# Clearing the convolution's input tile with GpSimd, and loading x for it in four transfers

## The chip, the cores and the metric

The kernel runs on one core of one Trainium2 chip. The metric is device microseconds of one execution, the median of several runs; lower is better.

## The reference

Two branches share the work, and a gate mixes them. `x` has 2048 rows of 448 channels, in bfloat16, and is the input of both; all weights are bfloat16.

```python
g = sigmoid((x * gate_w).sum(-1, keepdims=True))
# A: attention with 16 heads of 28, one key head and one value head for all
q = (x @ wq) -> 16 heads;  k = x @ wk;  v = x @ wv
p = softmax(q k^T * 28 ** -0.5);  a = (p v) @ wo
# B: a state-space convolution along the rows; 256 complex states for each channel
K[d, l] = Re(sum_n C[d, n] * exp(dt[d] * A[d, n] * l) * dt[d] * B[d, n])
y = causal convolution of x and K along l, by channel (the reference uses FFTs);  b = y + x * Dskip
out = g * a + (1 - g) * b
```

## The kernel before, in words

The attention runs as 1024 score tiles: 16 groups of 64 (a group is a block of 512 queries and 4 heads). For each tile TensorE makes 128 keys by 512 queries in PSUM (L1373 from four row strips, `qT`, or L1396 from the zero-padded copy `qM`). ScalarE takes the exponential of two or three tiles at once into the ring `expT` (L1428, 410 of them). TensorE then multiplies by the values into the bank `psB` (L1449, four tiles at a time). At a group's end VectorE copies `psB` to `acc` (L1173), and only then may the next group's first L1449 write the bank. TensorE also multiplies by zeros where it would be idle (L1349, L1355, L731).

The queries of each group are projected by TensorE (L893, L902) and moved out by VectorE (L899, L905); GpSimd issues four transfers that spread them from `qT` to `qM`.

The convolution runs beside this. VectorE squares complex numbers (the masters, L934 to L954) and builds tables of powers (L974 to L1024) in 14 chunks of 32 channels. TensorE makes the convolution's kernel from them (L1047), VectorE copies it to `kstg` (L1059), GpSimd stores it to DRAM (`KP`), and SyncE loads it back as shifted rows: the T loads, mostly into `T`. TensorE multiplies them with `U` (L1114); L1124, L1135 and L1144 turn the result, scale it and add it to `O`.

`U` holds the convolution's input for half of the channels at a time. Each pair of channels has 64 words of four bytes in each partition: the first 16 are rows of x (`in_A_x_dram` in the profile), the other 48 are the same rows moved by 32, 64 and 96 places, with zeros where nothing is moved in. So `U` is first cleared, then the input is loaded to the staging tile `O`, then VectorE copies it into `U` (and the second half of the channels into `T`) at L627, and then transfers from `U` to `U` (`ushift`, 24 issues) make the moved copies. After that a transfer clears `O`, which is used as the output's accumulator from then on.

All instructions are put into order by a planner in the kernel (`Prog.schedule`). Each step is an `op` (or a `dma`) with an engine, an assumed duration, the keys that it reads and writes, and a priority `pr`, lower first. The planner works through time and takes, over all engines, the step that can start first. So an edit in one step moves others on every engine. Waits come from the keys: the last writer of a key that is read, the readers of a key that is written. A `dma` waits for the one before it in the same slot. Steps in `late` may start only after the last store of the transposed x (`XS_scratch`). On GpSimd each computing step waits for the one before it. In the kernel before, `U`'s zero-fill has the key `Uz`, the two groups of eight loads have `("ust", 0)` and `("ust", 1)`, and the moved copies have `("Uc", c)` for a chunk c. All DMA issues have line 164 in the profile, where the helper `dma` records them.

Of the kernel before, what the change touches and what calls it, by code (L numbers as in the profile page):

```python
# [12 lines left out]
P = 128  # L13

S = 2048
D = 448
# [20 lines left out]
UA = D // 2  # L37
# [47 lines left out]
def dram(t, off, dims):  # L85
    return bass.AP(tensor=t.tensor, offset=t.offset + off, ap=[list(d) for d in dims])
# [342 lines left out]
class Kernel:  # L429
# [117 lines left out]
    def loads(self):  # L547
        pg, ins = self.pg, self.ins
        self.xst = self.tab
        x = ins["A_x"]  # L550

        def lx(q):
            pg.dma([(self.xst.v(0, P, q * QS, [[1, 4 * D]]), dram(x, q * 4 * P * D, [[4 * D, P], [1, 4 * D]]))],
                   (128, 3584), f"x{q}", wr=[("xst", q)], fac=0.85)
        self.raw = self.T
        self.late = []
        raw = self.raw
        names = ["B_A_im", "B_A_re", "B_B_re", "B_B_im", "B_C_re", "B_C_im"]

        def lraw(k, eng="sp"):  # L560
            pg.dma([(raw.v(0, DT, k * 1024, [[1, 1024]]), dram(ins[names[k]], 0, [[1024, DT], [1, 1024]]))],
                   (112, 2048), f"raw{k}", wr=[("raw", k)], eng=eng, fac=0.8)
        self.dtb = self.cst
        wst = self.mbf
        wks = self.seedw
        lx(0)
        pg.dma([(self.dtb.v(0, 1, 0, [[1, D]]), dram(ins["B_log_dt"], 0, [[D, 1], [1, D]]))], (1, 896), "ldt", wr=["dt"], eng="act", extra=-1500)
        pg.dma([(wks.v(0, DT, 0, [[1, 112]]), dram(ins["A_wk"], 0, [[112, DT], [1, 112]]))], (112, 224), "wk", wr=["wks"], eng="act")
        lx(1)
        lx(2)  # L570
        lraw(0)
        lx(3)
        pg.dma([(wst.v(0, DT, 0, [[1, 4 * D]]), dram(ins["A_wq"], 0, [[4 * D, DT], [1, 4 * D]]))],
               (112, 3584), "wq", wr=["wqs"], fac=0.85)
        pg.dma([(wks.v(0, DT, 112, [[1, 112]]), dram(ins["A_wv"], 0, [[112, DT], [1, 112]])),
                (wks.v(0, DT, 224, [[1, 4]]), dram(ins["gate_w"], 0, [[4, DT], [1, 4]]))],
               (224, 200), "wv", wr=["wvs"], extra=1500)
        lraw(1)
        pg.op("dve", lambda e: e.tensor_copy(self.Wk.v(0, DT, 0, [[32, 16], [1, DH]]),
                                             wks.v(0, DT, 0, [[DH, 4], [0, 4], [1, DH]])), 300, rd=["wks"], wr=["Wk"])  # L580
        pg.op("dve", lambda e: e.tensor_copy(self.Wq.v(0, DT, 0, [[32, 64], [1, DH]]),
                                             wst.v(0, DT, 0, [[DH, 64], [1, DH]])), 620, rd=["wqs"], wr=["Wq"])
        pg.op("dve", lambda e: e.tensor_copy(self.Wv.v(0, DT, 0, [[32, 4], [1, DH]]), wks.v(0, DT, 112, [[DH, 4], [1, DH]])),
              180, rd=["wvs"], wr=["Wv"], pr=0.3)
        pg.op("dve", lambda e: e.tensor_copy(self.Wv.v(0, DT, 28, [[32, 4]]), wks.v(0, DT, 224, [[1, 4]])),
              100, rd=["wvs"], wr=["Wvg"], pr=0.3)
        V0 = lambda b, off, n, r: b.v(0, P, off, [[n // r, r], [1, n // r]])
        Z = lambda n, r: self.cst.v(0, P, 512, [[0, r], [1, n // r]])
        uc = [("Uc", c) for c in range(14)]
        self.late.append(pg.dma([(V0(self.U, 0, 64 * UA, 64), Z(64 * UA, 64))], (8192, 448), "zU", rd=[("cst", 1)],  # L590
                                wr=["Uz"], pr=0.25).i)
        for k in range(2):
            lst = [(self.O.v(0, P, (8 * k + j) * D, [[1, D]]),
                    dram(x, 32 * (15 - 8 * k - j) * D, [[D, 32], [512 * D, 4], [1, D]])) for j in range(8)]
            self.late.append(pg.dma(lst, (1024, 896), f"u{k}", wr=[("ust", k)], pr=0.3).i)
        for k in range(2, 6):
            lraw(k)
        pg.dma([(V0(self.Wo, 0, NT * D, 8), Z(NT * D, 8))], (1024, 448), "zW", rd=[("cst", 1)], wr=["Wo"], pr=1)
        pg.dma([(self.k0.v(0, 1, 0, [[1, D]]), dram(ins["B_Dskip"], 0, [[D, 1], [1, D]]))], (1, 896), "sk", wr=[("kst", 1)], pr=1)
        w = ins["A_wo"]  # L600
        pg.dma([(self.Wo.v(32 * r, DH, 0, [[D, 4], [1, D]]), dram(w, DH * r * D, [[D, DH], [4 * DH * D, 4], [1, D]]))
                for r in range(4)], (448, 896), "wo", rd=["Wo"], wr=["Wo"], pr=2)
        pg.dma([(dram(self.KP, 2049, [[4 * KW, 112], [KW, 4], [1, 63]]), self.cst.v(0, 112, 512, [[64, 4], [1, 63]]))],
               (448, 126), "pad", rd=[("cst", 1)], wr=["pad"], pr=3)
# [10 lines left out]
    def prep_u(self):  # L615
        pg = self.pg
        done = []
        U4, T4, O4 = (b.cast(mybir.dt.int32) for b in (self.U, self.T, self.O))
        for half in range(2):
            for k in range(2):  # L620
                if half == 0:
                    dst, w = U4.v(0, P, 8 * k, [[64, UA // 2], [1, 8]]), ["Uz", ("Ub", k)]
                else:
                    dst, w = T4.v(0, P, UB // 2 + 8 * k, [[16, UA // 2], [1, 8]]), ["rawdone", ("UB", k)]
                key = ("ustd", half, k)
                done.append(key)
                pg.op("dve", lambda e, dst=dst, k=k, half=half: e.tensor_copy(  # L627
                    dst, O4.v(0, P, (8 * k * D + half * UA) // 2, [[1, UA // 2], [D // 2, 8]])), 1000,
                    rd=[("ust", k)] + ([] if half else []), wr=w + [key], pr=1 + half)
        for k, (c0, c1) in enumerate(((0, 2), (2, 5), (5, 9), (9, 14))):  # L630
            n = 16 * (c1 - c0)
            pg.dma(self.ushift(self.U, 1024 * c0, self.U, 1024 * c0, 128, n, 1), (6 * 16 * n, 64), f"du{k}", rd=[("Ub", 0), ("Ub", 1)],
                   wr=[("Uc", c) for c in range(c0, c1)], pr=0.35 if k < 2 else 0.9 + 0.1 * k, slow=True, iss=700.0)
        V0 = lambda b, off, n, r: b.v(0, P, off, [[n // r, r], [1, n // r]])
        Z = lambda n, r: self.cst.v(0, P, 512, [[0, r], [1, n // r]])
        pg.dma([(V0(self.O, 0, 16 * D, 32), Z(16 * D, 32))], (4096, 448), "zO", rd=[("cst", 1)] + done,
               wr=[(x, q) for q in range(16) for x in ("O", "Oz")], pr=1)
# [911 lines left out]
```

## Time and profile before

| what | value |
|---|---|
| median of 3 runs | 497.94 us (497.27 to 498.53) |
| profiled execution, span from the first to the last instruction | 498.77 us (the page rounds it to 498.8) |
| TensorE busy | 462.3 us (93%) |
| VectorE busy | 458.6 us (92%) |
| ScalarE busy | 484.0 us (97%) |
| GpSimd busy | 183.8 us (37%), nearly all of it issuing DMAs |
| granted TensorE clock, mean | 0.997 |

The profile is one execution; its own time is the span of its instructions, 0.83 us above the median of the runs, which were taken without a profile. A group's row in the page's part 5 gives busy time, mean duration of one in ns and, behind the second bar, the engine's idle time just before those instructions with the engine that ended most of it. A row of a timeline has the start, the busy time, the engine, the line, the operation and the tiles; equal instructions that follow each other are one row with a count, and brackets at the end give the idle time ahead of the row and what ended it. A row on "SPq" is SyncE's queue issuing, and its time is that of the issue alone.

### The profile page before, as it was taken

The numbers are of one execution on the slowest core, as the hardware profiler recorded it, in microseconds if no ns is written. First come the engines' busy times: TensorE is split into PE (matmuls) and PEld (weight loads), VectorE is DVE, ScalarE is ACT, GpSimd is POOL, SyncE is SP. The second block draws the span as 40 slices with busy tenths as digits, with TensorE's granted clock in tenths as the row PEclk, the third lists the DMA queues.
The fourth block names the chain that finished last, engine by engine and source line by source line (L and its number), as shares of the span: only waits on it lengthen the run. The fifth ranks groups of instructions, "written<-read, shape, count | busy, mean of one in ns | idle before, by whom it ended". The sixth has DMA issues, their size and how long they took to land.

```text
span 498.8 us, 17277 instructions
## 1 busy us (share of the span) xinstructions
PE 462.3 (93%) x7559; PEld 207.8 (42%) x7645; DVE 458.6 (92%) x872; ACT 484.0 (97%) x436; POOL 183.8 (37%) x331
## 2 busy tenths in 40 slices
PE   8899899999999999999999999999999999999997
PEld 5432233343443444444334344444534344444444
DVE  6998999999999999999999999999999999995224
ACT  6999899999999999999999999999999999999995
POOL 2102034225232527428616552643743525142110
PEclk9999899999999999999999999999999999999999
DMA  8996686935809555776942963798595695877752
GB/s 242 319 187 159 96 174 103 282 119 160 246 12 283 132 184 141 217 205 155 291 124 50 272 171 85 204 234 207 137 279 141 171 285 131 268 207 230 215 175 71
DMA packets 117479, 91.86 MB, mean 184 GB/s; under 512 B 48698, under 2 KB 112492, under 8 KB 117404
## 3 DMA queue, kind: packets, MB, share of 16 engines
q1 hardware_dynamic: 106746, 78.91, 57.7%
q0 software_dynamic: 10384, 11.70, 9.9%
q8 instruction: 60, 0.98, 0.9%
q10 hardware_dynamic: 274, 0.14, 0.1%
q14 instruction: 15, 0.12, 0.1%
HBM read 73.61 MB, written 5.23 MB: 158 GB/s over the span
## 4 chain that ended last, share of the span: by engine, by line
ACT 85%; SPq 6%; PE 4%; DVE 4%; DMA 1%; issue 0%
ACT expT L1428 84%; SPq L164 6%; DVE tab L988 1%; PE psS L658 1%; DMA O<-in_A_x_dram 1%; DVE tab L1003 0%; PE psS L1373 0%; PE psS L1396 0%; PE psS L1286 0%; PE psB L1349 0%; PE psB L1449 0%; ACT L805 0%; PE psS L1047 0%; DVE expT L680 0%; PE psX L1047 0%
## 5 line engine op out<-in xcount | busy, mean ns | idle before, releaser
L1428 ACT ACTIVATE expT<-psS 128x1536 bf16<-128x1536 f32 (+1 forms) x410 | 464.4, 1409 | 3.8 <-PE psS L1373 2.6
L988 DVE TENSOR_TENSOR tab<-tab,mbf 128x512 bf16<-128x512 bf16 (+4 forms) x140 | 139.4, 999 | 0.0
L1373 PE MATMUL psS<-qT,kT 29*128 29x512 bf16 x684 | 96.1, 386 | 12.0 <-ACT expT L1428 6.9
L1449 PE MATMUL psB<-expT,vaug 128*32 128x512 bf16 x1000 | 100.1, 390 | 2.2 <-DVE acc L1173 1.9
L1396 PE MATMUL psS<-qM,kT 128*128 128x512 bf16 x240 | 78.0, 382 | 13.8 <-issue 7.9
L164 POOL DMA_DIRECT2D KP_scratch<-kstg x104 | 57.1, 556 | 65.1 <-DVE kstg L1059 59.5
L1003 DVE TENSOR_TENSOR tab<-tab 128x256 bf16<-128x256 bf16 (+4 forms) x140 | 77.1, 571 | 0.0
L1449 PEld LDWEIGHTS psB<-expT,vaug 128*32 128x32 bf16 x1000 | 25.7, 93 | 74.9 <-issue 70.7
L164 POOL DMA_DIRECT2D qM<-qT x64 | 32.5, 516 | 59.0 <-DVE qT L905 38.4
L1373 PEld LDWEIGHTS psS<-qT,kT 29*128 29x128 bf16 x684 | 23.7, 91 | 64.3 <-ACT expT L1428 50.9
L164 POOL DMA_DIRECT2D U<-T x49 | 36.6, 750 | 36.2 <-DMA U<-T 14.6
L1355 PE MATMUL psB<-ident,one 128*128 128x512 bf16 x149 | 49.0, 389 | 0.0
L164 POOL DMA_DIRECT2D rdenB<-R_scratch x60 | 31.9, 538 | 34.6 <-DMA R_scratch<-denT 33.8
L1114 PE MATMUL psS<-T,U 128*26 128x128 bf16 (+3 forms) x1856 | 42.8, 221 | 0.5 <-issue 0.3
L1114 PEld LDWEIGHTS psS<-T,U 128*26 128x26 bf16 (+3 forms) x1856 | 32.9, 105 | 16.7 <-issue 11.7
L1017 DVE TENSOR_TENSOR tab<-tab,tmp 128x1984 bf16<-128x1984 bf16 x28 | 32.5, 1185 | 0.1
L1114 PE MATMUL psX<-T,U 128*32 128x128 bf16 (+3 forms) x1408 | 31.6, 221 | 0.0
L1396 PEld LDWEIGHTS psS<-qM,kT 128*128 128x128 bf16 x316 | 19.0, 97 | 30.1 <-ACT expT L1428 20.5
L164 POOL DMA_DIRECT2D denT<-acc x15 | 10.7, 716 | 55.8 <-DVE acc L1173 55.8
L1114 PEld LDWEIGHTS psX<-T,U 128*32 128x32 bf16 (+3 forms) x1408 | 24.3, 105 | 11.0 <-issue 7.4
L1011 DVE TENSOR_TENSOR tmp<-tmp,mq 128x64 bf16<-128x64 bf16 (+4 forms) x70 | 25.2, 360 | 0.0
L934 DVE TENSOR_TENSOR msq<-seedz 128x512 f32<-128x512 f32 (+1 forms) x40 | 24.6, 616 | 0.0
(188 smaller groups left out, 502.9 us busy)
## 6 DMA issues: line engine op xcount, KB each, us to landing
T<-KP_scratch SPq DMA_DIRECT2D x204, 272.0 KB, 4.9
U<-KP_scratch SPq DMA_DIRECT2D x20, 272.0 KB, 6.2
rdenB<-R_scratch POOLq DMA_DIRECT2D x60, 64.0 KB, 3.6
U<-cst SPq DMA_DIRECT2D x1, 3584.0 KB, 25.2
qM<-qT POOLq DMA_DIRECT2D x64, 32.0 KB, 3.7
tab<-in_A_x_dram SPq DMA_DIRECT2D x4, 448.0 KB, 5.3
O<-in_A_x_dram SPq DMA_DIRECT2D x16, 112.0 KB, 3.0
O<-cst SPq DMA_DIRECT2D x1, 1792.0 KB, 9.3
```

The source lines that it names most:

```text
L164: return [e.dma_start(o, i, **kw) for o, i in pairs]
L934: pg.op("dve", lambda e: e.tensor_tensor(m2(msq), z2, z2, ALU.mult), el(2 * n), rd=[kr, ki] + first, wr=["msq"], pr=pr)
L988: mul = lambda e, o, a, b: e.tensor_tensor(o, a, b, ALU.mult)
L1003: vo(lambda e, dv=dv, tv=tv, k=k: e.tensor_tensor(dv, dv, tv, ALU.add if k else ALU.subtract), n, [kt[k], kd[k]], [kd[k]], 1.92 if lv else ...
L1011: vo(lambda e, w=w, lv=lv: e.tensor_tensor(rho.v(0, P, (32 - 2 * w) * 2, [[64, 32], [2, w], [1, 2]]), rho.v(0, P, (32 - w) * 2, [[64, 32], ...
L1017: vo(lambda e, k=k: e.tensor_tensor(tab.v(0, P, FM + k * FP + 2, [[64, 32], [2, 31], [1, 2]]), tab.v(0, P, lm + k * PL + 62, [[64, 32], [- ...
L1114: r = e.matmul(ps.v(32 * j, 32 - m0, 128 * k, [[1, 128]]), self.U.v(0, P, (4 * gi + j) % UA // 2 * 128 + 2 * (2 * m0 + par) + j % 2, [[4, ...
L1355: return e.matmul(t.v(0, P, off, [[1, 512]]), self.one.v(0, P, 2, [[0, P]]), self.ident.v(0, P, 0, [[0, 4], [1, P]]), start=b != 6, stop=b ...
L1373: r = e.matmul(self.psS.v(0, P, 512 * b, [[1, 512]]), kT.v(32 * h, DH + 1, 128 * kt, [[1, 128]]), qT.v(32 * h, DH + 1, 512 * (i % 2), [[1, ...
L1396: return e.matmul(self.psS.v(0, P, 512 * b, [[1, 512]]), kT.v(0, P, 128 * kt, [[1, 128]]), self.qM.v(0, P, (i % 2) * XQ + 512 * h, [[1, 51 ...
L1428: o = pg.op("act", lambda e: e.activation(expT.v(0, P, 512 * es[0], spread(es, n)), self.psS.v(0, P, 512 * bs[0], spread(bs, n)), AF.Exp, ...
L1449: r = e.matmul(self.psB.v(32 * h, 32, 0, [[1, 512]]), vaug.v(0, P, 32 * kt, [[1, 32]]), expT.v(0, P, 512 * ring[t], [[1, 512]]), start=(kt ...
```

## The change

The zero-fill transfer of `U` is taken out. In its place GpSimd clears 14 pieces of `U`, each 8 pairs of channels, and of each pair only the 48 words that VectorE's copy doesn't write. The pieces have the keys `("Uc", c)`, which the moved copies write later. The sixteen transfers of x, one for each column block of `O`, become four, one for each residue of the partition number modulo four: 32 partitions with 16 rows of 448 channels. All four copies at L627 wait for all four transfers. The bytes that are loaded, their place in `O` and the rest of the kernel are the same. Lines behind the edit have numbers higher by one in the changed kernel.

```diff
         V0 = lambda b, off, n, r: b.v(0, P, off, [[n // r, r], [1, n // r]])
         Z = lambda n, r: self.cst.v(0, P, 512, [[0, r], [1, n // r]])
-        uc = [("Uc", c) for c in range(14)]
-        self.late.append(pg.dma([(V0(self.U, 0, 64 * UA, 64), Z(64 * UA, 64))], (8192, 448), "zU", rd=[("cst", 1)],
-                                wr=["Uz"], pr=0.25).i)
-        for k in range(2):
-            lst = [(self.O.v(0, P, (8 * k + j) * D, [[1, D]]),
-                    dram(x, 32 * (15 - 8 * k - j) * D, [[D, 32], [512 * D, 4], [1, D]])) for j in range(8)]
-            self.late.append(pg.dma(lst, (1024, 896), f"u{k}", wr=[("ust", k)], pr=0.3).i)
+        U4 = self.U.cast(mybir.dt.int32)
+        for c in range(14):
+            pg.op("pool", lambda e, c=c: e.memset(U4.v(0, P, 512 * c + 16, [[64, 8], [1, 48]]), 0), 470.0, wr=[("Uc", c)], pr=4)
+        for h in range(4):
+            xs = 4 * self.O.rs
+            pg_pair = (bass.AP(tensor=self.O.h, offset=h * self.O.rs, ap=[[xs, 32], [D, 16], [1, D]]),
+                       dram(x, (512 * h + 32 * 15) * D, [[D, 32], [-32 * D, 16], [1, D]]))
+            self.late.append(pg.dma([pg_pair], (512, 896), f"u{h}", wr=[("ust", h)], pr=0.3).i)
...
                 if half == 0:
-                    dst, w = U4.v(0, P, 8 * k, [[64, UA // 2], [1, 8]]), ["Uz", ("Ub", k)]
+                    dst, w = U4.v(0, P, 8 * k, [[64, UA // 2], [1, 8]]), [("Ub", k)]
...
-                    rd=[("ust", k)] + ([] if half else []), wr=w + [key], pr=1 + half)
+                    rd=[("ust", h) for h in range(4)], wr=w + [key], pr=1 + half)
```

## The prediction

> **What bounds the kernel now.** I read the page's chain of work first, then ScalarE's costliest group in its part 5.
>
> ```profile
> ACT 85%; SPq 6%; PE 4%; DVE 4%; DMA 1%; issue 0%
> L1428 ACT ACTIVATE expT<-psS 128x1536 bf16<-128x1536 f32 (+1 forms) x410 | 464.4, 1409 | 3.8 <-PE psS L1373 2.6
> ```
>
> The 410 exponentials of the attention take 464.4 us on ScalarE, and ScalarE is idle before them for only 3.8 us. So a change can do three things to the time: move the start of this stream, close part of the 3.8 us, or open new gaps. Next, ScalarE's timeline, to see where the 3.8 us lie; the number in brackets is the idle time before the row.
>
> ```profile
> 31.71 2.37 ACT L1428 ACTIVATE expT<-psS 128x1536 bf16<-128x1536 f32 x2 [0.72 <-PE psS L1396]
> 34.23 24.27 ACT L1428 ACTIVATE expT<-psS 128x1536 bf16<-128x1536 f32 x21 [0.16 <-PE psS L1396]
> 59.45 1.02 ACT L1428 ACTIVATE expT<-psS 128x1024 bf16<-128x1024 f32 x1 [0.95 <-PE psS L1373]
> 61.51 2.52 ACT L1428 ACTIVATE expT<-psS 128x1536 bf16<-128x1536 f32 x2 [1.03 <-PE psS L1373]
> 64.39 4.62 ACT L1428 ACTIVATE expT<-psS 128x1536 bf16<-128x1536 f32 x4 [0.36 <-PE psS L1373]
> ```
>
> Two further gaps, 0.23 us at 69.2 and 0.26 us at 80.9, are the last; from 80.9 to 492.0 us nothing starves ScalarE. Everything lost is lost in the first 81 us, where the change lies. Why TensorE was late is in the timelines of SyncE's queue, VectorE and TensorE:
>
> ```profile
> 15.42 1.64 SPq L164 DMA_DIRECT2D U<-cst  x1
> 17.11 31.53 SPq L164 DMA_DIRECT2D O<-in_A_x_dram  x16
> 50.92 0.95 DVE L627 COPY U<-O 128x896 int32<-128x896 int32 x1 [2.99 <-DMA O<-in_A_x_dram]
> 57.93 0.70 DVE L1173 COPY acc<-psB 128x512 f32<-128x512 f32 x1
> 58.69 0.40 PE L1449 MATMUL psB<-expT,vaug 128*32 128x512 bf16 x4 [1.94 <-DVE acc L1173]
> ```
>
> The zero-fill keeps the DMA engines busy, and the first load of x, issued at 17.1, holds the queue 20.7 us. The sixteenth lands at 50.9. VectorE stands 2.99 us for it; all behind it is late, also the copy that frees psB (L1173); TensorE stands 1.94 us for that copy. The windows by five microseconds show what follows (PEclk is third from the end):
>
> ```profile
> 55.00:60.00 5.00, 3.06 (x21) 1.00 (x22) 5.00 (x11) 4.05 (x4) 0.71 (x1) 0.97 0.52 59
> 60.00:65.00 5.00, 4.85 (x26) 1.20 (x26) 5.00 (x7) 3.56 (x4) 0.00 (x0) 0.69 0.95 199
> ```
>
> After its stand TensorE is granted 0.69 of its clock, and that is where the gaps of 1.03 and 0.36 us come from. The gap at 31.7 has another cause. The trace gives its releaser as ScalarE, which had long been done; the answer for tile qM in the window 20.5 to 24 has the real one:
>
> ```profile
> L164 POOL DMA_DIRECT2D qM<-qT x4: 496/496/672, 21.0 to 22.7; - x4
> DMA to landing us min/median/max: 5.7/5.8/8.1
> ```
>
> The last of these four issues, at 22.7, lands 8.1 us later at 30.8, just when TensorE loads its first weights for L1396 (30.83). The next four, at 40.5 us without the zero-fill, land in 2.3 to 2.6 us.
>
> **The change, part by part.** *Removed: the zero-fill.* Its 3584 KB land 25.2 us after issue. Without it the loads of x come right behind the three XS stores (issued last at 14.6, landing after 6.6 to 7.5 us, so at 21.2 to 22.1).
>
> *x in four transfers.* Same 1.84 MB, same 896-byte rows, 4 issues in place of 16; SyncE is through at about 18 us instead of 48. When does the last one land? In the window 40 to 45 us the loads of x moved 223 GB/s at a DMA share of 0.83, so 269 GB/s at a full share: 6.8 us. From 21.4 that is 28.2, and with the 3.0 us from issue to landing of one of these loads as an outer allowance, 31.2. The slow bound is the pace of the sixteen (12 issues in 7.8 us, 177 GB/s): 10.4 us, landing at 34.8. I take 30 to 32.
>
> *VectorE's order.* The listing of the changed program puts the four copies L627 directly behind the second seedw product, which ends at 31.7; in the kernel before they start at 44.9 and 50.9. The first copy now waits for all four transfers. Queued behind it: the reduction L899 for the second q projection, the k0 row (L878) and the whole chain of masters. If x is there at 31.7, the 2.99 us are gone. Up to the copy L1173 the list is otherwise the same plus one small product L1011 (0.13 us apart in the trace): 31.69 + (57.93 - 31.69) - 2.99 + 0.13 = 55.07, done at 55.77. TensorE came to the waiting L1449 at 58.69 - 1.94 = 56.75, now 0.88 us sooner (next item), so at 55.87: no stand, no slow clock. A late x has cover: 1.94 us of standing became a gap of 0.95, so 1.0 us of standing costs nothing directly, and x may land up to about 32.8.
>
> *qM.* The loads of x are out of the DMA engines some 9 us sooner than the zero-fill, so the qM transfers issued at 21.0 to 22.7 should land by 30.3, when TensorE is free (L1349 ends at 30.30): the gaps of 0.72 and 0.16 us close, 0.88. Bounds: 0 if they still take 8.1 us, 0.88 if the 5.8 of their median.
>
> *GpSimd's 14 clears.* Each is 128x384 words of four bytes. Rows of this trace:
>
> ```profile
> 1.34 0.21 POOL L511 MEMSET kstg<- 128x128 f32 x1
> 1.97 0.09 POOL L511 MEMSET expT<- 28x1 bf16 x1
> ```
>
> So 0.12 us for 127 more words, 0.36 for 383 more, 0.45 for one; with 0.07 us between two, 14 take 7.3 us, from 4.5 to 11.8. GpSimd's next work is the qM issue at 21.0, after 16.28 us of idling: that idling hides them; even at twice the length they end at 19. The first shift transfers (U<-U) wait for GpSimd and VectorE, both long done. What they can cost is VectorE's start-up. No row shows GpSimd computing beside a copy between two SBUF tiles on VectorE. Bounds: nothing, or one clear's 0.45 us ahead of each of L579 (5.77), L808 and L831 (11.58). Of the first two's 0.90, TensorE's wait for ScalarE hides 0.49 (VectorE's first xT copy ends at 7.53, L688 starts at 8.06 after ScalarE's at 8.02); the rest, 0.41, passes to kT, L696 and, with L831's 0.45, through L832 to ScalarE's L834, behind which ScalarE is full until the first exponential: 0.86 at most. Nothing here can gain. I take 0.43, the middle.
>
> [...]
>
> *Moved.* The shifts U<-U go from 51.9 to 79 us to about 34 to 53, and the k0 store behind them; the first reader, the convolution's L1114, starts at 96.9, and the first T load at 84.0, so both hide. If the shifts slow the qM transfers at 40.5 to 8 us, their first reader is at 65.0: hidden. Further on the planner has re-ordered all engines (ScalarE's order is the same); I count nothing for that, and keep it as rivals.
>
> **Sum.** Closed: 0.88 + 0.95 + 1.03 + 0.05 (a small one at 63.0) + 0.36 = 3.27 us. Start-up: 0.43 lost. Net 2.84 us. The profiled span of 498.77 becomes 495.93; it lies 0.83 above the median of the runs, 497.94, so the forecast is 495.1 us.
>
> **Rivals.**
> 1. *x still comes late, or one new stand eats the gain* (0.24). At the slow bound, 34.8 us, VectorE stands 3.1 us at 31.7 instead of at 47.9: the gaps at 59 to 64 stay, only qM's 0.88 less 0.43 remains: 497.5. For it: the margin is 1 to 2 us, and a transfer lands with its slowest DMA engine. Against it: the sixteen were paced by issues, at a share under 0.86. A single later stand as long as the present one (2.39 us of gap) also gives 497.5.
> 2. *The new order makes TensorE stand at later changes of the head group* (0.20): slower. Place: the psB copy L1173, which occurs 15 times, each time VectorE's list is a microsecond or two late beside a product of 1.1 to 2.3 us. Price: 2.39 us each by the row at 58.7. From two of them on the gain is gone: 497.94 - 2.84 + 4.78 = 499.9. Against it: in the kernel before, 14 of 15 cost nothing, and all 56 T loads after 80 us landed before use. For it: TensorE's products often end within 0.1 us of the exponential that needs them, so there is little to absorb a bad order.
> 3. *The clears do not run where they seem to.* The listing has all 14 ahead of GpSimd's first DMA; only a clear above 1.1 us would delay qM. I give it no share of its own.
>
> **Chances.** 0.3% (1.5 us) is about what a measurement can tell from no change. Forecast, below 496.4: 0.56, its own range 494.1 (all gaps closed, no start-up cost: 3.8 us off) to 496.4. Within: 0.24. Slower: 0.20. Range for 8 in 10: 494.1 to 499.9, which takes in rival 1 and the near part of rival 2.
>
> **What would show it.** Right: no VectorE idle time before the L627 copies (now at about 32), L1173's copy near 55 and no TensorE stand behind it, PEclk 1.00 from 60 to 65, ScalarE idle before exponentials under 1 us in total, the first exponential at 21.3 to 22.1. Wrong at x: a DMA wait of 2 us or more before L627 at 32. Wrong at start-up: a first exponential after 22.1. Wrong altogether: ScalarE gaps of over 2.8 us in total after 81 us.

## The result, and the profile after

| what | before | changed |
|---|---|---|
| median of 4 runs each, same chip | 497.75 us (497.27 to 498.53) | 504.36 us (501.44 to 506.81) |
| span of the profiled execution | 498.77 us | 504.8 us |
| mean granted TensorE clock of the profiled execution | 0.997 | 0.982 |
| ScalarE idle before the exponentials | 3.8 us | 6.6 us |

The ratio is 1.0128, with a 95% interval of 1.0079 to 1.0176. The forecast was 495.1 us, with 499.9 as its upper end. Medians here and below are over all executions of a kernel; ratios and their intervals leave out executions more than 1.5% above their kernel's fastest.

The first 81 us went as forecast. In VectorE's timeline the copies of x start at 31.70 and the copy that frees psB at 55.02, without a wait for x:

```profile
31.70 1.81 DVE L628 COPY U<-O 128x896 int32<-128x896 int32 x2
...
55.02 0.69 DVE L1174 COPY acc<-psB 128x512 f32<-128x512 f32 x1 [0.22 <-PE psB L1450]
```

In ScalarE's timeline the first exponential starts at 21.26, and up to 68 us only two gaps of over 0.1 us are left:

```profile
21.26 1.44 ACT L1429 ACTIVATE expT<-psS 128x1536 bf16<-128x1536 f32 x1
...
33.52 31.97 ACT L1429 ACTIVATE expT<-psS 128x1536 bf16<-128x1536 f32 x28 [0.16 <-PE psS L1397]
65.72 3.71 ACT L1429 ACTIVATE expT<-psS 128x1536 bf16<-128x1536 f32 x3 [0.23 <-PE psS L1374]
```

The loss is at the other end. The page's clock row falls in the last two slices, and the exponentials' row has more idle time than before, now ended by L1385, a score product of the last head groups:

```profile
PEclk9999999999999999999999999999999999999966
...
L1429 ACT ACTIVATE expT<-psS 128x1536 bf16<-128x1536 f32 (+1 forms) x410 | 465.0, 1393 | 6.6 <-PE psS L1385 5.6
```

ScalarE's timeline from 475 us shows each gap. The last two rows are in the tail, where the results go out.

```profile
475.37 4.80 ACT L1429 ACTIVATE expT<-psS 128x1536 bf16<-128x1536 f32 x4
481.99 2.37 ACT L1429 ACTIVATE expT<-psS 128x1536 bf16<-128x1536 f32 x2 [1.81 <-PE psS L1385]
484.62 2.59 ACT L1429 ACTIVATE expT<-psS 128x1536 bf16<-128x1536 f32 x2 [0.27 <-PE psS L1385]
488.31 1.45 ACT L1429 ACTIVATE expT<-psS 128x1536 bf16<-128x1536 f32 x1 [1.10 <-PE psS L1385]
490.19 1.02 ACT L1429 ACTIVATE expT<-psS 128x1024 bf16<-128x1024 f32 x1 [0.43 <-PE psS L1385]
492.10 1.45 ACT L1429 ACTIVATE expT<-psS 128x1536 bf16<-128x1536 f32 x1 [0.88 <-PE psS L1385]
494.66 0.60 ACT L1429 ACTIVATE expT<-psS 128x512 bf16<-128x512 f32 x1 [1.11 <-PE psS L1385]
499.67 0.38 ACT L1243 ACTIVATE acc<-psB 32x256 f32<-32x256 f32 x1 [4.41 <-PE psB L1444]
502.00 0.54 ACT L1310 ACTIVATE O<-psS 128x448 bf16<-128x448 f32 x1 [1.95 <-PE psS L1287]
```

The six gaps before exponentials add up to 5.60 us. TensorE's timeline shows what came ahead of the first of them: a stand of 1.85 us that no engine and no transfer of the kernel ended ("issue").

```profile
478.99 0.47 PE L1115 MATMUL psX<-T,U 128*32 128x128 bf16 x17
481.31 0.30 PE L1115 MATMUL psX<-T,U 128*28 128x128 bf16 x7 [1.85 <-issue]
```

The windows around it have, behind the length, the busy time of TensorE, of its weight loads, of VectorE, ScalarE and GpSimd, then TensorE's granted clock, the DMA share and GB/s. Over the 3.41 us to 483.49 TensorE is busy for 2.18 us; from then on its clock is half.

```profile
476.66:480.08 3.42, 2.61 (x60) 1.17 (x53) 1.11 (x2) 3.42 (x4) 0.00 (x0) 1.00 0.92 250
480.08:483.49 3.41, 2.18 (x43) 0.96 (x46) 0.00 (x0) 1.60 (x3) 0.00 (x0) 1.00 0.06 18
483.49:486.90 3.41, 3.41 (x52) 1.22 (x56) 1.45 (x3) 3.03 (x3) 0.00 (x0) 0.50 0.00 0
```

The counts tie the stand to the arrival of instructions. The profile's queue "q8 instruction" moves 60 packets with 0.98 MB together, 16 KB each, and TensorE has 15,334 records in the trace: 255.6 for each packet. Numbered by their starts, the only two stands of over 0.5 us ahead of TensorE's products that are put down to "issue" (0.57 us at 177.33, 1.85 us at 481.31) are both at place 193 of 256, 41 times 256 records apart. A block, here, is 256 such records; that one packet brings one block is my reading of these counts. The block before the second one began at 474.29; the next packet of q8 started 4.5 us later, at 478.82, took 1.06 us, and TensorE went on 1.43 us behind its end.

### The profile page after: what moved, and what is told of

Read it like the earlier page. It is cut to its first block, busy times and chain, and to the rows that moved or that the text cites. A ratio compares the mean times of both kernels' runs of the same rounds, so it can differ in the third digit from the quotient of the medians.

```text
span 504.8 us, 17352 instructions
## 1 busy us (share of the span) xinstructions
PE 481.7 (95%) x7637; PEld 210.0 (42%) x7637; DVE 459.1 (91%) x872; ACT 484.6 (96%) x436; POOL 189.6 (38%) x345
## 4 chain that ended last, share of the span: by engine, by line
ACT 86%; PE 8%; issue 1%
ACT expT L1429 86%; PE psX L1115 1%; PE psS L1385 1%; PE psS L1397 1%; PE psS L1374 1%; PE psB L1444 1%; PE psS L1259 1%; PE psB L1350 1%; PE psB L1450 0%; PE psS L1234 0%; PE psS L1219 0%; PE psS L1287 0%; PE psX L1048 0%; PE psS L1048 0%; PE psS L894 0%
## 5 line engine op out<-in xcount | busy, mean ns | idle before, releaser
L1397 PE MATMUL psS<-qM,kT 128*128 128x512 bf16 x316 | 95.2, 384 | 0.8 <-ACT expT L1429 0.3
L1356 PE MATMUL psB<-ident,one 128*128 128x512 bf16 x141 | 46.4, 384 | 0.0
L1115 PE MATMUL psS<-T,U 128*26 128x128 bf16 (+3 forms) x1920 | 42.8, 221 | 0.1
L1115 PEld LDWEIGHTS psS<-T,U 128*26 128x26 bf16 (+3 forms) x1920 | 32.8, 105 | 16.1 <-issue 10.8
L1115 PE MATMUL psX<-T,U 128*32 128x128 bf16 (+3 forms) x1344 | 31.6, 223 | 2.4 <-issue 2.4
L1115 PEld LDWEIGHTS psX<-T,U 128*32 128x32 bf16 (+3 forms) x1344 | 23.6, 106 | 14.2 <-issue 10.0
```

Of the source, the lines that this page charges most:

```text
L1115: r = e.matmul(ps.v(32 * j, 32 - m0, 128 * k, [[1, 128]]), self.U.v(0, P, (4 * gi + j) % UA // 2 * 128 + 2 * (2 * m0 + par) + j % 2, [[4, ...
L1356: return e.matmul(t.v(0, P, off, [[1, 512]]), self.one.v(0, P, 2, [[0, P]]), self.ident.v(0, P, 0, [[0, 4], [1, P]]), start=b != 6, stop=b ...
L1397: return e.matmul(self.psS.v(0, P, 512 * b, [[1, 512]]), kT.v(0, P, 128 * kt, [[1, 128]]), self.qM.v(0, P, (i % 2) * XQ + 512 * h, [[1, 51 ...
```

## The experiments

Theory 1: the new order, which the planner made because of the edit, costs the time, by the late block and the half clock behind it. Theory 2: the edit itself costs it (GpSimd's clears beside VectorE, the four transfers). Theory 3: the half clock at the end comes without the stand, for want of work.

**Another order at the end (a_fetch).** One constant of the planner, the time after which the next block is taken to be there:

```diff
-    else self.FETCH if r < self.QUIET else self.IDLE))
+    else 7400.0 if 468000.0 < r < 474000.0 else self.FETCH if r < self.QUIET else self.IDLE))
```

> The changed kernel with one constant of its planner altered for one place: the block of TensorE instructions that is fetched for 476 us is taken to come 7.4 us after the one before it, where 4.8 us was assumed and the trace of the changed kernel shows 7.02 us (474.29 to 481.31). Only the order at the end of TensorE's list and a few VectorE rows change; GpSimd, SyncE and ScalarE keep theirs. Theory 1 (the loss is TensorE's late instruction block at 479 to 481 us, and the half clock that comes behind it): the 1.85 us stand goes, the half clock of 17.07 us shrinks to the three or four us that the kernel before has, ScalarE's gaps behind 480 us (6.6 us at the exponentials) fall to under 1 us, and the time is 494.5 to 498. Theory 2 (the clears and the x transfers themselves cost it): 501 to 507. Theory 3 (the half clock at the end comes without the stand, for want of work): the stand goes, the half clock stays, 500 to 504.

504.08 us, ratio 1.0103 (1.0057 to 1.0149). The stand at 481 is gone (behind 178 us none that is put down to "issue" is above 0.4), and so is the half clock of 17.07 us. But a half clock of 6.83 us now lies at 375.98, and in the tail ScalarE waits 4.94 us ahead of L1310 in place of 1.95, because the planner moved work there: convolution products (L1115) now run from 494.7 to 496.2 us, behind the last exponential. Theory 1's mechanism held and its time did not: one repair bought other losses. Theory 3's half clock at the end did not stay.

**The same order, blocks shifted (b_shift64, b_shift160).** In the emitting loop, waits that are met long before, 61 in one kernel (limit 64) and 155 in the other (limit 160), each one more instruction:

```diff
+    if e == "pe" and o.end > 100000.0 and extra < 64 and waits and "dve" not in waits:
+        waits = dict(waits, dve=1)
+        extra += 1
```

> The changed kernel in its own order, with 61 waits on VectorE that are long met added to TensorE instructions behind 100 us, each one instruction more, so that TensorE's blocks of 256 instructions end 61 instructions earlier in the work than in the changed kernel. Theory 1: the place where the block ends moves by about a quarter of a block, so the stand of 1.85 us at 481.31 changes in size or is gone, and the time moves with it by 2 us or more, to 495 to 500 if it is gone. Theory 2 and 3: the same 501 to 507 as the changed kernel, since order, clears and transfers are the same.

> As the kernel with 61 added waits, but with 155, so that the blocks of 256 instructions end 155 instructions earlier. Theory 1: the stand at 481.31 is gone or elsewhere, and the time differs from the changed kernel's by 2 us or more, 495 to 500 if no stand falls behind 470 us. Theory 2 and 3: 501 to 507.

500.62 us, ratio 1.0040 (1.0014 to 1.0066), and 500.96 us, ratio 1.0054 (1.0030 to 1.0079). The stand near 480 shrank to 0.57 and 1.06 us, with no half clock behind it in either trace. Order, clears and transfers are those of the changed kernel, so Theory 2 can't explain the 3.4 to 3.7 us that the median fell. What is left lies over other late blocks (0.80 us at 327 in the one, 1.12 us at 451.64 in the other) and half clocks in 10 of the 20 executions.

**Both edits in the old order (c_order).** GpSimd clears, x in four transfers; the planner sees the old costs, and a transfer of 128 bytes to a scratch tensor takes the zero-fill's place in the plan. The first copy also waits for both groups of loads, which the lines shown leave out:

```diff
+    z = pg.dma([(dram(self.ZZ, 0, ...), self.cst.v(0, 1, 512, [[1, 64]]))], (8192, 448), "zU", ..., wr=["Uz"], pr=0.25)
...
+    o = pg.dma(lst, (1024, 896), f"u{k}", wr=[("ust", k)], pr=0.3)
+    o.iss *= 4
```

> The changed kernel's two edits in the order of the kernel before: GpSimd clears U in 14 pieces, the one zero-fill transfer is replaced by one of 128 bytes into a scratch tensor, x comes in four transfers, and the planner is given the old costs, so that TensorE's list is that of the kernel before but for a few filler rows. Theory 1 (the edit itself gains what the prediction summed, and the new order loses it at 481 us): no stand at 480 us, the early gaps of ScalarE closed (3.3 us in the sum), 494 to 496.5 against 497.5 of the kernel before. Theory 2 (the clears and the transfers cost the time): slower than the kernel before, 500 or more. Theory 3: as before or up to 500, with the half clock at the end.

498.07 us, ratio 0.9997 (0.9975 to 1.0020): neither a gain nor a loss, and a mean clock of 0.999 or 1.00 in all ten executions. In its trace ScalarE's early gaps are 0.16, 0.23 and 0.26 us, so x came in time; a block came late there too (1.82 us at 475.46; ScalarE lost 1.60 us by it in this execution, the slowest of the ten), without a half clock. Theory 2 falls, and so does half of Theory 1's expectation: the early gain isn't there.

**The kernel before, once more (before_2).** No edit.

> The kernel before once more, for a second trace. The prediction took the profiled execution (span 498.77 us) as an ordinary one that lies 0.83 us above the median of the times; but the times of the changed kernel lie 1.72 us above their spans, by which the execution with a span of 498.77 would have taken 500.5 us, some 2.8 us above the median of 497.7. Theory A (the profiled execution was an unusual one): in this trace the half clock of 3.41 us at 59.7 us is absent, and ScalarE's gaps of 0.95, 1.03 and 0.36 us at 59 to 64 us add up to under 1 us, with a span of 495.5 to 496.5 us. So 1.5 to 2.3 us of the 2.4 us that the prediction counted as the gain at that place were not there to be gained. Theory B (it was ordinary): the same gaps, 2.3 to 2.5 us in total, whatever the span.

Span 496.6 us, time 498.36 us. Theory A holds, and more so than expected. ScalarE's timeline and VectorE's copies:

```profile
33.52 31.97 ACT L1428 ACTIVATE expT<-psS 128x1536 bf16<-128x1536 f32 x28 [0.16 <-PE psS L1396]
65.72 11.40 ACT L1428 ACTIVATE expT<-psS 128x1536 bf16<-128x1536 f32 x10 [0.23 <-PE psS L1373]
77.39 5.98 ACT L1428 ACTIVATE expT<-psS 128x1536 bf16<-128x1536 f32 x5 [0.27 <-PE psB L1449]
```

```profile
44.67 0.95 DVE L627 COPY U<-O 128x896 int32<-128x896 int32 x1
...
47.65 0.96 DVE L627 COPY U<-O 128x896 int32<-128x896 int32 x1
```

The gaps at 33.52 and 65.72 are those of the changed kernel to the hundredth. Neither copy waits: the loads of x were issued from 15.63 to 44.49 here, from 17.11 to 48.64 in the first profile. The stand of 1.94 us, its half clock and the gaps of 0.95, 1.03 and 0.36 us are in the first profile alone. Over the runs of the kernel before beside these experiments, 81 of 86 executions had a mean clock above 0.998; four had 0.990 to 0.997, a range in which the first profile's 0.997 lies, and one of 660.82 us had 0.559.

The gap of 0.72 us ahead of L1396 is another matter, and the other traces show it. Six traces are of kernels that keep the zero-fill (two of the kernel before, and n_null1, n_null2, g_gaps and d_cross, which are told further down). In three of them the last of the first four qM transfers lands at 30.28 to 30.73 us, and ScalarE has a gap of 0.72, 0.58 (n_null1, with a clock of 1.00) and 0.29 us (d_cross) there; in the other three it lands by 29.95 and there is none. In the eleven traces with GpSimd's clears it lands by 29.88, always without the gap. VectorE's wait for x also comes back, 1.56 us in n_null1, but there no gap of ScalarE follows at 59 to 64 us.

**The changed kernel, once more (after_2).** No edit.

> The changed kernel once more, for a second trace and more times. Theory 1 (late instruction block, then half clock): a stand of TensorE behind no other engine of 1 to 2.5 us at 479 to 482 us in this execution too, 500 to 507 us; executions whose mean clock is 1.00 are at 499 to 501.5, those at 0.98 at 504 or more, so that some 2 us of the loss come from the stand and the order and the rest from the half clock. Theory 2 and 3: the time is spread without a tie to the mean clock, or the stand is absent and the time the same.

504.44 us, ratio 1.0124 (1.0088 to 1.0161). The late block is there again (1.23 us at 483.64), with a half clock of 6.83 us from 484.93; another of 6.83 us starts at 375.70. Over the seven executions of the changed kernel that the ratios use, the times lie along 499.0 us + 423 us x (1 - mean clock), with a correlation of 0.97. Their mean clock is 0.9884: by this fit 4.9 us of the loss go with the half clock. The other 1.5 us, from 497.5 to 499.0, fit the late blocks and the tail; no run here separates these two.

**The new order without the edit's direct part (d_cross).** The changed kernel's plan, with the zero-fill and sixteen loads executed in it; GpSimd's pieces shrink to one element of a small tile.

```diff
-    pg.op("pool", lambda e, c=c: e.memset(U4.v(0, P, 512 * c + 16, [[64, 8], [1, 48]]), 0), 470.0, wr=[("Uc", c)], pr=4)
+    pg.op("pool", lambda e, c=c: e.memset(self.small.v(0, P, 4, [[1, 1]]), 0.0), 470.0, wr=[("Uc", c)], pr=4)
+    z = pg.dma([(V0(self.U, 0, 64 * UA, 64), Z(64 * UA, 64))], (8192, 448), "zU", rd=[("cst", 1)], wr=["Uz"], pr=0.25)
+    z.ns, z.iss = 1.0, 0.0
```

> The other way round from the kernel with the order of the kernel before: the order that the planner made for the changed kernel (TensorE's list differs in 7 rows), but with the direct parts of the kernel before. U is zeroed by the one transfer of 8192 descriptors, the 14 GpSimd pieces shrink to memsets of one element of a small tile, and x comes in sixteen transfers. Theory 1 (the order makes the loss): slow like the changed kernel or slower, 501 to 508, with a late block at 474 to 482 us and the early gaps at 31 us and behind it back. Theory 2 (the clears and the four transfers make it): as the kernel before, 497 to 498.5.

516.56 us, ratio 1.0400 (1.0355 to 1.0444). The late block is there (1.66 us at 501.02, this trace being some 20 us late), so it belongs to the order. The size was missed: VectorE's row shows why.

```profile
49.89 0.93 DVE L633 COPY U<-O 128x896 int32<-128x896 int32 x1 [18.14 <-DMA O<-in_A_x_dram]
```

The new order puts the copies at 31.7 and everything for the second q projection behind them; with x at 49.9, ScalarE stood for 15.10 us. In the changed kernel the last load of x lands at 27.98 us, 21.9 us earlier than here, and the copies start 18.2 us earlier. So the edit does deliver x early. The old order simply did not need it earlier.

**The old order with both edits and shifted blocks (c_shift64).** The 61 waits of b_shift64 in c_order.

> The kernel with both edits in the order of the kernel before, with 61 waits that are long met added on TensorE behind 100 us, so that its blocks of instructions end 61 instructions earlier. In the trace of the kernel without them, a block came 5.42 us late and TensorE stood for 1.82 us at 475.46. Theory 1: the stand there shrinks or moves; if none of over 0.5 us is left behind 400 us, the median falls from 498.07 to 496 to 497, below the kernel before. Against it: the transfers of 466 to 479 us fill the DMA engines, so another block may come as late; then 497.5 to 499. Theory 2: no change from 498.

499.48 us, ratio 1.0052 (1.0032 to 1.0071): a miss for both theories' numbers, and nearest to the sentence against it. The stand at 475 is gone, but a block now comes 1.54 us late at 326.25, and ScalarE loses 1.00 us there. The old order is exposed too. In before_2 its blocks come late by stands of 0.47 us at 326.48, 0.56 at 467.39 and 0.59 at 473.72, for which ScalarE loses 0.17, 0.17 and 0.43 us; it happens to lie well.

**New plans for old work (n_null1, n_null2, m_replan).** Only a figure that the planner assumes is altered: 620 to 720 ns for the copy of Wq in the kernel before and in the changed kernel, 1000 to 900 ns for the copies of x in the kernel before.

```diff
-    wst.v(0, DT, 0, [[DH, 64], [1, DH]])), 620, rd=["wqs"], wr=["Wq"])
+    wst.v(0, DT, 0, [[DH, 64], [1, DH]])), 720, rd=["wqs"], wr=["Wq"])
```

> The kernel before with nothing of its work altered: only the planner is told that one early VectorE copy (the one of Wq, L581) takes 720 ns in place of 620. The instructions are the same, their order is planned anew (1395 lines of TensorE's list differ). Theory 1 (it is the order that came out of the planning that costs the changed kernel its time, so any new planning draws a new order and new late stands): the time moves by more than 0.3%, somewhere between 496 and 504, and the trace shows stands of TensorE of over 0.6 us at other places than the kernel before. Theory 2 (the clears and the transfers cost it): within 0.3% of the kernel before, 496 to 499.

> As the run before it, with another figure altered: the planner is told that the four copies of x (L627) take 900 ns in place of 1000 (the trace shows 945 to 960). Theory 1: a third order with a time of its own between 496 and 504, different from the run before it. Theory 2: 496 to 499.

> The changed kernel with the same false figure for the copy of Wq, so that the same work as in the changed kernel is planned into another order. Theory 1: the time leaves the 504.4 of the changed kernel by 2 us or more, to 496 to 502, and the stand at 479 to 484 us is another or gone. Theory 2: 503 to 505.5 again, since clears and transfers are the same.

n_null1: 499.80 us (497.62 to 503.71), ratio 1.0049 (1.0023 to 1.0075). n_null2: 498.94 us, ratio 1.0037 (1.0013 to 1.0061), with a late block of 1.59 us at 326.87 in its trace. The work is that of the kernel before; only the order differs, and with it the number of dummy products at L1355 (156 in before_2's trace, 157 and 159 in these). Both are slower, by 0.49% and 0.37%, with intervals clear of 1, though n_null2's 498.94 lies in the ranges of both theories. n_null1's trace is of one of its fastest executions (497.85 us) and has neither a late block of over 0.4 us nor a half clock, so what its slower executions lost by isn't shown. m_replan: 503.92 us (499.45 to 508.56), ratio 1.0075 (1.0042 to 1.0109). That is where Theory 2 had it, and its interval overlaps that of the changed kernel, so by the time alone it decides little; its trace, of its fastest execution, has late blocks at 449.77 (0.66 us) and 480.72 (1.10 us).

**Less traffic at the end (t_less).** The last four loads of T bring one row block of eight, and the kernel leaves the rest out:

```diff
+    nr = 1 if gi >= 52 else 8
...
-    lst.append((to, dram(self.KP, h * 512 + 1 + 8 * gi * KW, [[1, 32], [KW, 8], [1, TC]])))
+    lst.append((to, dram(self.KP, h * 512 + 1 + 8 * gi * KW, [[1, 32], [KW, nr], [1, TC]])))
```

> The changed kernel in its own order, but the last four of the 56 loads of T (issued at 462 to 474 us) bring one eighth of their rows, so seven eighths of the input of the last convolution blocks are left out. Theory 1 in its finer form (TensorE's instruction block comes late because its 16 KB wait in DMA engines that the loads of T fill): the fetches between 466 and 480 us begin within 1.5 us of the block before them in place of 2.5 to 4.6 us, TensorE's stand at 481 to 484 us is gone, no half clock begins at 479 to 485 us, and the median falls from 504.4 to 499 to 502 (the half clock that sometimes begins at 375 us stays). Against it: the fetch is late for another reason, then the stand stays and the time is 503 to 505.5.

499.64 us, ratio 1.0031 (1.0017 to 1.0045). Two windows of the same four microseconds, the changed kernel first (columns as above):

```profile
474.00:478.00 4.00, 3.81 (x103) 1.92 (x104) 0.69 (x1) 4.00 (x5) 0.00 (x0) 1.00 1.08 306
```

```profile
474.00:478.00 4.00, 3.78 (x105) 1.91 (x102) 0.69 (x1) 4.00 (x4) 0.00 (x0) 1.00 0.15 30
```

The DMA share falls from 1.08 to 0.15; behind 178 us no stand of TensorE of over 0.4 us is put down to "issue" any more, and from 478.08 ten exponentials follow each other without a gap. So here the loads of T make the block late; when each packet was asked for isn't in the trace. The kernel before was not run with these loads cut, so a part of the gain may be one that it would have too: in before_2 ScalarE loses 0.60 us behind the late blocks at 467.39 and 473.72. Seven of ten executions still had a mean clock below 0.998.

**The half clock (f_fill, f_fill_tless, g_gaps).** One product of TensorE is issued three times ahead of the 0.63 us stand at 375 us, in the changed kernel and in the one with less traffic. The third kernel is the kernel before, with 16 dummy products cut to 4 columns:

```diff
+    for _ in range(2 if e == "pe" and j == 1709 else 0):
+        o.fn(x)
```

```diff
+    self.tiny = e == "pe" and o.i >= self.nops and 264000.0 < o.end < 279000.0
...
+    if getattr(pg, "tiny", False):
+        return e.matmul(t.v(0, P, off, [[1, 4]]), self.one.v(0, P, 2, [[0, P]]), self.ident.v(0, P, 0, [[1, 4]]), ...)
```

> The changed kernel in its own order, with one product of TensorE (L904, planned at 373 us) issued three times in place of once, just ahead of the stand of 0.63 us at 375 us that ends at ScalarE. It costs no other engine anything, and fills that stand. Theory G (the half clock begins at the end of a step of 3.41 us in which TensorE stood for some 0.8 us or more, by chance of where the steps lie): no half clock begins at 375 to 380 us any more, the one at 479 to 485 us stays, so the mean clock rises and the median falls from 504.4 by 0.5 to 2.5 us, to 502 to 504. Rival (the half clock comes at its own times, whatever TensorE does there): half clocks as before, 503.5 to 505.5.

> The same filling of the stand at 375 us, in the kernel whose last four loads of T bring one eighth of their rows (seven eighths of the input of the last convolution blocks are left out), which had a median of 499.64 and a mean clock of 0.990 to 0.997 in seven of its ten executions. Theory G: with both stands gone hardly an execution has a half clock, the mean clock is 0.998 or more, and the median falls to 498.2 to 499.0, which is the 498.6 that a straight line through those ten times against their clocks gives at clock 1. Rival: 499.3 to 500 with the same clocks.

> The kernel before in its own order, with the 16 dummy products of TensorE (L1355) that are planned between 264 and 279 us cut from 512 columns to 4, so that TensorE stands for 0.7 to 1.2 us in each step of 3.41 us there, all of it in waits for ScalarE that cost ScalarE nothing; no other work is altered and no order. Theory G: half clocks appear between 268 and 290 us that the kernel before does not have, the mean clock falls to 0.98 to 0.997, and the time rises by 0.4 us for each us of half clock, to 499 to 503. Rival (a half clock needs a late block, a late transfer or the end of the kernel): clock 1.00 and 497 to 498 as the kernel before.

f_fill: 503.19 us (498.94 to 509.39), ratio 1.0072 (1.0039 to 1.0105). No half clock at 375 in its trace; the late block (1.52 us at 480.69) and a half clock of 17.07 us from 482.86 are there. By its time it is only a hint, since the interval overlaps that of the changed kernel. f_fill_tless: 497.46 us, ratio 0.9993 (0.9977 to 1.0009); two of ten executions below 0.998, where t_less had seven. With both stands gone, and seven eighths of those loads left out, the new order takes the time of the kernel before (by the interval within 0.3%), under the 498.2 that was expected.

g_gaps: all ten executions have a mean clock of 0.992 to 0.997, where 22 of 25 of the kernel before beside it had more than 0.998. Its windows, and those of the kernel before (before_2), in steps of 3.41 us:

```profile
270.75:274.16 3.41, 2.53 (x21) 0.93 (x22) 3.41 (x3) 3.41 (x5) 3.41 (x6) 1.00 0.96 287
274.16:277.57 3.41, 3.08 (x18) 1.02 (x16) 3.41 (x5) 3.41 (x4) 1.29 (x3) 0.50 1.12 247
277.57:280.98 3.41, 3.36 (x50) 1.37 (x52) 3.41 (x10) 3.28 (x4) 2.24 (x3) 0.50 1.11 261
```

```profile
270.75:274.16 3.41, 3.32 (x21) 0.83 (x21) 3.41 (x3) 3.41 (x5) 3.41 (x6) 1.00 0.86 240
274.16:277.57 3.41, 3.32 (x19) 1.11 (x18) 3.41 (x5) 3.41 (x4) 1.48 (x3) 1.00 1.13 259
```

Here the stands alone (2.53 us of work in the step to 274.16, in place of 3.32) bring the half clock. The other direction, taking it away by filling a stand, rests on fewer numbers: the trace of f_fill, and two executions of ten in place of seven. The price was over-estimated: 498.80 us, ratio 1.0020 (1.0002 to 1.0038), since at that place ScalarE lost only 0.79 us for 6.83 us of half clock. At the end of the changed kernel it lost 3.79 us (the five gaps behind 484 us) for 17.07, and more in the tail: its waits there of 4.41 and 1.95 us are 2.37 and 1.55 in b_shift64, which has the same order at a full clock.

## Why the prediction was wrong

*The base was an unusual execution.* The step that failed first is "it lies 0.83 above the median of the runs". Times lie some 1.7 us above their spans (506.52 to 504.8, 498.36 to 496.6), so the span of 498.77 stood for about 500.5 us, 2.8 above the median. What made it unusual is most of the 3.27 us that the sum closes: 0.72, 0.95, 1.03, 0.05 and 0.36, all but a gap of 0.16. In an ordinary execution (before_2) only 0.16 + 0.23 of that stretch up to 68 us is left, and the changed kernel has the same two. Against before_2 the gain to be had was at most the 0.27 us of the gap at 77.39, and against an execution with a late qM 0.3 to 0.7 us more; c_order measured no gain, with an interval that would hide one of up to 1.2 us.

*Moved: "I count nothing for that".* This is the step that turned a gain into a loss: the re-ordering cost 1.3%. With the edit in the old order the ratio is 0.9997; new orders without any edit cost 0.4 and 0.5%, so order alone can cost time, and this one cost more. It worked through a mechanism that no rival had, a late instruction block; the planner's FETCH of 4.8 us was in view, and the real distance was 7.02 us (474.29 to 481.31). Rival 2 had the sign and the right sort of cause, a bad order, at the wrong place: no stand of over 0.4 us behind L1174 is left. Of the loss, 4.9 us went with the half clock, which the prediction knew at 59.7 us but priced only as something to gain.

*x in four transfers, VectorE's order.* Right: the copies at 31.70 without a wait, L1174 at 55.02 where 55.07 was worked out, no stand behind it. The last load of x landed at 27.98, earlier than the 30 to 32 that I took and near the 28.2 worked out from a full share. The slow last part that rival 1 speaks of shows in this load: fourteen of its sixteen completions come by 26.13 us, the last two at 27.69 and 27.98. *qM.* The mechanism was right and its size was not: the slowest transfer lands 6.7 us behind its issue in place of 8.1 and the gap of 0.72 is gone, but 0.16 stays, and before_2, with 7.3 us, has no gap of 0.72 either.

*The clears and the start-up.* GpSimd's rows end at 11.75 where 11.8 was estimated. The copy L579, which meets a clear, takes 0.51 us in place of 0.28 (VectorE's rows, the kernel before first):

```profile
5.77 0.28 DVE L579 COPY expT<-seedw 112x448 bf16<-112x448 bf16 x1 [1.93 <-DMA seedw<-in_A_wk_dram]
```

```profile
5.81 0.51 DVE L579 COPY expT<-seedw 112x448 bf16<-112x448 bf16 x1 [1.98 <-DMA seedw<-in_A_wk_dram]
```

At VectorE's next instruction, L809, it is the clear that takes longer: L809 starts at 6.24 and takes 0.37 us where it took 0.38, and the clear that starts beside it takes 0.73 us in place of 0.42. L832 (L831 before) takes 0.66 us where it took 0.63. That one clear's 0.45 us comes ahead of each of these three was my estimate, and no run shows it, nor the 0.43 us that rests on it: the first exponential starts at 21.26, and at 21.25 in before_2, so 0.01 arrived.

*The mark "wrong altogether"* was met: behind 81 us the gaps before exponentials are 5.60 us plus 0.19 at 178, above the 2.8 that were named.

## What to carry to other kernels

Before a gap is counted as a gain, compare the profiled execution with the runs by the same quantity: its span against their spans, its clock against theirs. A gap that comes with a clock below that of most runs (here 0.997, where 81 of 86 executions had more than 0.998) is probably not in the median. Where a planner or scheduler re-orders behind an edit, price the re-ordering by planning the old work anew (one assumed duration altered); here that alone moved the time by 0.4 to 0.5%, more than the edit had to give. And a stand of TensorE that costs nothing by itself may still be paid for later, by the clock: in g_gaps ScalarE lost 0.79 us in the 6.83 us of half clock behind such stands.

## What the runs showed of the hardware

*The half clock.* Its pieces ahead of the end are 3.41 us long in the first profile, 6.83 in a_fetch, after_2 and g_gaps, and 17.07 in the changed kernel and f_fill, and in three traces they start whole multiples of 3.413 us apart (483.49 and 503.97 in the changed kernel: six; 375.70 and 484.93 in after_2: 32; 59.69 and 500.01 in the first profile: 129). A step, here, is one such stretch of 3.41 us. Eight half clocks began at the end of a step in which TensorE was busy for 1.47 us (the first profile), 2.18 (the changed kernel), 2.60 and 2.19 (after_2), 2.44 (a_fetch), 2.61 (b_shift160), 2.53 (g_gaps) and 2.17 (f_fill). In the fullest of these steps it stood for 0.80 us in all:

```profile
198.93:202.34 3.41, 2.61 (x24) 0.79 (x21) 3.41 (x6) 3.41 (x4) 0.71 (x1) 1.00 0.29 77
202.34:205.75 3.41, 3.41 (x43) 1.20 (x43) 2.63 (x6) 3.14 (x4) 1.99 (x4) 0.50 0.82 244
```

These are windows of b_shift160. Most such steps don't do it. With the steps of all 17 traces laid out from their half clocks, 32 steps at full clock between 30 and 485 us have 2.61 us of work or less, and 10 of them are followed by a half clock. The changed kernel's profile has four of the 32, with 2.52 us of work from 200.18, 2.53 from 374.26, 2.61 from 476.66 and 2.18 from 480.08, and only the last of them has a half clock behind it. In n_null2 the clock stayed whole behind a step with 1.66 us of work:

```profile
324.90:328.31 3.41, 1.66 (x60) 1.03 (x62) 3.41 (x5) 2.15 (x3) 1.23 (x2) 1.00 1.11 307
328.31:331.72 3.41, 3.36 (x45) 1.34 (x34) 3.41 (x4) 3.41 (x4) 1.27 (x3) 1.00 1.00 286
```

What decides between the two, and why it lasts from one step to five, stays open.

*The instruction block.* In the changed kernel's profile TensorE has 255.6 records for each 16 KB packet of q8. In the two stands at 177.33 and 481.31, work went on 1.42 and 1.43 us behind the packet's end. While the loads of T filled the DMA engines (share 1.08 from 474 to 478 us, 0.92 from 476.66 to 480.08), a packet started 4.5 us behind the beginning of the block before it (478.82 and 474.29). In t_less, with a share of 0.15 from 474 to 478 us, the late block there is gone.
